# Attention and two squared-ReLU/mish MLPs on one core: tau and the first queries through ScalarE's queue, and a new written-out order

## The chip, the cores and the metric

The program runs on one core of a Trainium2 chip. The metric is device time in microseconds (us) of one execution; lower is better. The profile's engines are PE (TensorE), PEld (its weight loads), DVE (VectorE), ACT (ScalarE), POOL (GpSimd) and SP (SyncE, which here only issues DMAs). SPq and ACTq are the DMA issues in those engines' instruction streams.

## The reference

```python
# attention: 4 batches, 8 heads, 576 positions, head size 64
scores = scale * q @ k.T
scores = where(scores >= max(scores) - tau, scores, -1e9)     # tau = 0.02
attn = softmax(scores) @ v                                    # eps 1e-9 in the sum
x = attn as 2304 rows of 512
# first MLP, 512 -> 2048 -> 512
r = maximum(x @ w_in, 0);  x = (r * r) @ w_out
# second MLP, 512 -> 2048 -> 512
h = x @ w_in2;  out = (h * tanh(softplus(h))) @ w_out2
```

The inputs of the MLPs' weights are 64-bit floats, which the kernel reads as pairs of 32-bit words and takes apart into a high and a low 32-bit part.

## The kernel before, in words

Attention works on pairs of heads, four pairs in a batch, sixteen in all. A pair is of kind "d" (direct, fp32 throughout: all four of batch 0 and the first of batch 1), "h" (direct scores, values in two fp16 parts) or "s" (everything in two fp16 parts; ten pairs). `job_direct` loads a direct pair's k and q with two or three DMAs each, turns them on PE (the line L860 transposes into a PSUM tile `s`), and copies them to SBUF (L871 on ACT, L873 on DVE). `job` does the same for an "s" pair: its loads of k and q are of the kind "n4", four DMAs each (L768, L770), into the buffers `f0` to `f2`, and its turns are DMA transposes (L488). `unit` takes two head tiles of scores: matmuls L491 into `s0` and `s1`, then on DVE `top` (L936), which scales by `cd` and finds the maximum, then `most` (n<-m, L946 on ACT, L951 on DVE), then exp on ACT, with the mask either on ACT (L973 and L977) or on DVE (L984 and L989). `cd` comes from tau through `consts` (L509 to L515 on DVE). In the fp16 pairs the weights of the attention go to `pt` by a DMA transpose (`pt<-hl`, L488) and the values' matmul is `small<-V,pt`.

The attention's rows go to DRAM (xs: `xdr<-xx`, L1160) and come back as the MLP's blocks (xl: `xx<-xdr`, L1249). There are nine blocks of 256 rows. The first MLP of seven blocks runs between the attention's units; from about 500 us on PE does MLP work alone. The weights of the first MLP are loaded by `weights` (L548, L556) and converted by five to seven operations for each half: `size` L581, `rest` L593, `clamp` L588, `shift` L605, `sign` L611 (or, where `sp` says so, `factor` and `times`), `to_hi` and `to_lo` (L650).

Nothing of the order is left to the framework. Every operation and every DMA is put into a `Plan` with its possible engines, their costs, its dependencies and a due time. `Plan.order` runs a list scheduling forwards and backwards `fbi` times over a model of the engines, and the kernel issues everything in the order of the starts so found; each engine then runs its own instructions in that order and waits at each for what it needs. The parameters in `PAR` and `BIAS` set due times (`cd`, `blk`, `off`, `ahead`), which spare places are used (`ex`, `exo`), how a choice of engine is biased (`BIAS`), how late a load is taken to land after its issue (`land`), when PE prefers to stay with fp16 or fp32 (`stayt`, `stay`), and which queues a kind of DMA may use (`on`: S for SP, A for ACT). `LOADS` holds each kind's issue cost in each queue. `warm` puts up to eight matmuls of `ones` into PE's gaps at the start. `pm` says how many of nine score tiles have their mask on ACT, for each batch.

Of the kernel before, what the change touches and what calls it, by code (L numbers as in the profile page):

```python
# [24 lines left out]


PAR = dict(
    on=dict(n3="S", n4="S", x2="A", xl="SA", xs="A"),
    merge=8,
    warm=(1, 0, 7),  # L30
    won=("S", "S"),
    land=1.963,
    lag=0.625,
    turns=("h", "s0"),
    kv=(("nat0", "V1"), ("f1", "nat1"), ("KT1", "f0"), ("V0", "KT0")),
    cd=(-308.461, 3.819, -131.904),
    urg=-14.633,
    rawt=-5.99,
    kinds="dddd",
    cgen=4.726,  # L40
    split=(),
    ex=dict(cw=3, cr=2, raw=37, pd=6, sc=1),
    exo=("sc", "cr", "cw", "pd", "raw"),
    blk=list((8.563, 55.919, 139.126, 253.351, 384.4, 475.303, 619.227, 867.985, 1044.55)),
    tb2=83.369,
    down2=308.21,
    sp=(0, 4),
    off=(175.279, 19.269, 48.635, -244.561, 181.854, 84.18, -264.447, -32.298),
    ahead=(25.339, 120.493, 7.244, -166.185, 20.703, 130.933, 10.735, 565.487, 305.271, -75.571),
    start=-133.597,  # L50
    area=dict(sc=("x0", "x1"), hl=("x2",)),
    jobahead=21.48,
    fbi=7,
    stay=1.5,
    stayt=150.0,
    kinds2="ssss",
    kb=("dhss", "ssss", "ssss"),
    pm=(9, 9, 3, 0),
    tmax=0.75,
    pstay=4.0,  # L60
    proom=0.7,
)


# [20 lines left out]
class Plan:  # L85
# [3 lines left out]


    TABLE = 1.3
    BIAS = {"V": 2.013, "A": 1.855, "P": 2.0, "S": 0.46}
    SHARE = 0.8
    FIRST = 0.4
    TICK, ENTRY = 3.4133, 1.275
# [21 lines left out]
    def op(self, opts, fn, r=(), w=(), x=(), due=0.0, load=None, tab=None, two=False, half=0):  # L117

        o = Op()
        o.two, o.half, o.bank = two, half, 0  # L120
        for b in (*r, *w, *x):
            o.bank |= b.bank
        o.opts, o.fn, o.due, o.load, o.tab, o.n = opts, fn, due, load, tab, len(self.ops)
        deps = set()
        for b in r:
            assert b.wr and not b.gone, "read before written or after its place's next use"
            deps.update(b.wr)
            b.rd.append(o.n)
        for b in w:
            for z in b.prevs:  # L130
                deps.update(z.users())
            b.wr.append(o.n)
        for b in x:
            deps.update(b.users())
            b.wr.append(o.n)
        deps.discard(o.n)
        o.deps = deps
        self.ops.append(o)
        return o
# [77 lines left out]
    def forwards(self, succ):  # L217
# [29 lines left out]
        while count < len(ops):  # L247
            best = None
            for e in engs:
# [8 lines left out]
                for _, n in now:  # L258
                    o = ops[n]
                    if len(o.opts) > 1:  # L260
                        bias = self.BIAS
                        mine = t + o.opts[e] + bias[e]
# [110 lines left out]
def attention_moe_moe_kernel(ctx: ExitStack, tc: tile.TileContext, q, k, v, tau, w1i, w1o, w2i, w2o, out):  # L373
    nc = tc.nc
    B, H, S, D = q.shape
# [15 lines left out]
    tt = sb.tile([128, 6], F32, name="tt", tag="tt")  # L391
    cd = sb.tile([128, 8], F32, name="cd", tag="cd")
# [28 lines left out]
    def sbuf(place, shape, dt):  # L421
        if place in AREA or place in HALF:
            base, z, whole, over = HALF[place] if place in HALF else ("area", *AREA[place])
            n = min(whole, math.prod(shape[1:]) * (2 if dt == F16 else 4) // 4)

            def make():
                t = within(base, SIZE[base])[:, z:z + n]
                t = t if dt == I32 else t.bitcast(dt)
                if len(shape) == 4:
                    return t.rearrange("p (a b c) -> p a b c", b=shape[2], c=shape[3])  # L430
                return t.rearrange("p (a b) -> p a b", b=shape[2]) if len(shape) == 3 else t

            return plan.buf(place, make, over=over)
        return plan.buf(place, lambda: sb.tile(shape, dt, name=place, tag=place))
# [24 lines left out]
    def rot(*places):  # L459
# [5 lines left out]

    LOADS = {
        "n4": (dict(S=2.95, P=2.75, A=1.9), 1.86, 0.8, 1.9),
        "d3": (dict(S=2.05, P=2.1), 1.3, 0.5, 1.2), "d2": (dict(S=1.4, P=1.5), 0.65, 0.5, 0.8),
        "q1": (dict(S=0.75, P=0.8), 0.0, 0.4, 0.4), "q2": (dict(S=1.45, P=1.4), 0.62, 0.19, 0.65),
        "w8": (dict(S=0.6, P=0.9, A=0.5), 0.0, 3.4, 3.2),  # L470
        "w": (dict(S=0.6, P=0.75, A=0.45), 0.0, 1.8, 1.42), "n3": (dict(S=2.3, P=2.0, A=1.4), 1.24, 0.9, 1.6),
        "n2": (dict(S=1.45, P=1.35), 0.62, 0.5, 1.4),
        "tau": (dict(S=0.5, P=0.6), 0.0, 0.2, 0.2),
        "xs": (dict(S=0.72, P=0.65, A=0.5), 0.0, 0.36, 0.36), "tail": (dict(S=1.6, P=1.3), 0.6, 0.19, 0.38),
        "xl": (dict(S=0.63, P=0.56, A=0.45), 0.0, 0.55, 0.5), "x2": (dict(S=0.6, P=0.56, A=0.45), 0.0, 0.75, 0.7),
        "xr": (dict(S=0.45, P=0.56), 0.0, 0.64, 0.64), "out": (dict(S=0.45, A=0.45), 0.0, 0.65, 0.65),
# [3 lines left out]
    def dma(fn, kind, r=(), w=(), x=(), due=0.0, on=None):  # L480

        cost, *load = LOADS[kind]
        on = on or PAR["on"].get(kind, "S")
        op({e: cost[e] for e in on}, lambda e: fn({"S": nc.sync, "A": nc.scalar, "P": nc.gpsimd}[e]), r, w, x, due,
           load=load)
# [10 lines left out]
    blk = PAR["blk"]  # L496
    blk = blk + [blk[-1] + PAR["tb2"] * (n + 1) for n in range(NB + 1)]
# [6 lines left out]
    K, K0, KI, KT_ = (plan.buf(z, lambda: None) for z in ("const", "ones", "ident", "tau"))  # L504
# [10 lines left out]
        nc.vector.tensor_copy(out=cd[:, 3:4], in_=tt[:, 0:1])  # L515


    dma(lambda e: e.dma_start(out=tt[:, 3:4], in_=tau.to_broadcast([128, 1])), "tau", w=[KT_], due=-40.0)
    op({"V": 0.45}, consts, r=[KT_], w=[K], due=-39.0)

    W = {}
# [306 lines left out]
    def job_direct(p, due):  # L828

        keep = p.keep  # L830
        p.c, p.cv = K, None
        p.QT = sbuf(rot("Q0", "Q1"), [128, 576], F32)
        todo = [(q, p.QT, 6, p.tiles)]
        if keep is not None and "KT" in keep:
            p.KT = keep["KT"]
        else:
            p.KT = sbuf(rot("KT0", "KT1") if keep is None else PAR["kv"][p.h0 // 2][0], [128, 576], F32)
            todo.insert(0, (k, p.KT, 6.5, (0, 5)))
        for x, dst, z, (j0, j1) in todo:
            src = x[p.b, p.h0:p.h0 + 2]  # L840
            raw = sbuf(rot(*(spare["raw"] if not p.late else ("f0", "f1", "f2"))), [128, 5, 2, 64], F32)
            main = min(j1, 4)

            def load(e, raw=raw, x=src, j0=j0, j1=j1, main=main):
                for h in range(2):
                    e.dma_start(
                        out=raw()[:, j0:main, h, :],
                        in_=x[h, 0:512, :].rearrange("(p j) d -> p j d", j=4)[:, j0:main, :],
                    )
                if j1 == 5:  # L850
                    e.dma_start(out=raw()[0:64, 4, :, :], in_=x[:, 512:576, :].rearrange("h p d -> p h d"))

            dma(load, "d3" if main - j0 == 4 else "d2", w=[raw], due=due - 9 - z)
            o = pbuf(place("s", "s0", "s1"), [128, 1024])
            cols = slice(128 * j0, min(576, 128 * j1))

            def turn(e, raw=raw, o=o, j0=j0, j1=j1):
                for j in range(j0, j1):
                    n = 128 if j < 4 else 64
                    nc.tensor.transpose(  # L860
                        o()[:, 128 * j:128 * j + n], raw()[0:n, j].rearrange("p h d -> p (h d)"), ident[0:n, 0:n]
                    )

            t = op({"T": 0.15 * (j1 - j0)}, turn, r=[raw, KI], w=[o], due=due - z)
            if len(turns) < 2:
                turns.append(t)
                warm(len(turns), t)

            def evac(e, dst=dst, o=o, cols=cols):
                if e == "A":  # L870
                    nc.scalar.activation(out=dst()[:, cols], in_=o()[:, cols], func=AF.Copy)  # L871
                else:
                    nc.vector.tensor_copy(out=dst()[:, cols], in_=o()[:, cols])  # L873

            n = cols.stop - cols.start
            op({"A": 0.11 + 0.42 * n / 576, "V": 0.1 + 0.6 * n / 576}, evac, r=[o], w=[dst], due=due - z + 1 - URG)

        if keep is not None and "V" in keep:
            p.V = keep["V"]
            return  # L880
        if p.kind == "h":
            return job_v(p, due)
        p.V = V = sbuf(rot("V0", "V1") if keep is None else PAR["kv"][p.h0 // 2][1], [128, 10, 64], F32)
        if keep is not None:
            keep.update(KT=p.KT, V=p.V)


        def load_v(e):
            r = V().rearrange("p (h j) d -> p h j d", h=2)
            vv = v[p.b, p.h0:p.h0 + 2]  # L890
            e.dma_start(
                out=r[:, :, 0:4, :].rearrange("p h j d -> p h (j d)"),
                in_=vv[:, 0:512, :].rearrange("h (p j) d -> p h (j d)", j=4),
            )
            e.dma_start(out=r[64:128, :, 4, :], in_=vv[:, 512:576, :].rearrange("h p d -> p h d"))

        dma(load_v, "n2", w=[V], due=due - 8)
# [727 lines left out]
    with tc.manual_schedule():  # L1625
        made, code = {}, nc.cur_bb.bb.instructions
        followed = {o.after for o in plan.ops if o.after is not None}
        for n in seq:
            o = plan.ops[n]
            z = len(code)  # L1630
# [39 lines left out]
```

## Time and profile before

| | |
|---|---|
| time, median of 3 runs | 1012.12 us (1010.97 to 1012.97) |
| profiled execution | 1012.55 us, of which the span of its instructions is 1010.8 us |
| PE busy | 987.2 us, 98% of the span |
| DVE, ACT, POOL busy | 649.6, 523.8 and 86.4 us |
| mean granted clock of PE | 0.997 |

The span runs from the first to the last instruction; 1.75 us lie around it. Busy time of PE counts matmuls whose ends are modelled, and issuing a DMA does not count as busy time of the engine that issues it.

### The profile page before, as it was taken

Reading aid. Unit: us, or ns where it says so; the run is one execution under the profiler, and the core shown is the slowest. Engines: PE = TensorE matmul, PEld = TensorE weight load, DVE = VectorE, ACT = ScalarE, POOL = GpSimd, SP = SyncE. Lnnn points to the kernel's source line nnn. Section 1 sums busy time; section 2 is a strip of 40 time slices with the busy share of each in tenths; the row PEclk is TensorE's granted clock in tenths of the full one; section 3 lists DMA queues with packets and bytes.
Section 4 is the critical chain, followed back from the end, with each engine's and each line's share of the span. In section 5 each row is a group of like instructions: output and inputs, shape, how many; then the busy total and the mean of one; then the engine's idle time right before and its main releaser. Section 6 shows DMA issues by size and latency. Waiting matters only on the chain.

```text
span 1010.8 us, 20772 instructions
## 1 busy us (share of the span) xinstructions
PE 987.2 (98%) x8191; PEld 863.4 (85%) x8191; DVE 649.6 (64%) x1486; ACT 523.8 (52%) x978; POOL 86.4 (9%) x120
## 2 busy tenths in 40 slices
PE   6899999999999999999999999999999999999998
PEld 4577799889888898998999888888888888888997
DVE  4999999888898897889855799943223122222222
ACT  5899988867777665766544578611111120111111
POOL 1344312100000100110001000000000000000000
PEclk8999999999999999999999999999999999999999
DMA  7635667897978797779852345401011010010001
GB/s 206 201 119 161 200 130 159 159 162 152 177 142 153 145 171 144 139 158 150 158 163 78 108 153 172 168 1 42 1 42 42 0 42 1 21 42 1 1 12 51
DMA packets 231185, 109.43 MB, mean 108 GB/s; under 512 B 194608, under 2 KB 212016, under 8 KB 231088
## 3 DMA queue, kind: packets, MB, share of 16 engines
q1 hardware_dynamic: 219504, 98.93, 43.7%
q10 hardware_dynamic: 11584, 9.18, 2.9%
q8 instruction: 64, 1.05, 0.4%
q14 instruction: 33, 0.27, 0.1%
HBM read 58.16 MB, written 14.16 MB: 72 GB/s over the span
## 4 chain that ended last, share of the span: by engine, by line
PE 80%; DMA 4%; SPq 2%; DVE 1%; ACT 1%; issue 0%; ACTq 0%
PE s L491 27%; PE acc L491 24%; PE h L491 19%; PE small L491 9%; DMA pt<-hl 2%; SPq L488 1%; DMA f<-in_q_dram 1%; SPq L770 1%; SPq L768 0%; DMA pt<-area 0%; PE s L1254 0%; DMA xx<-xdr 0%; DVE gl L650 0%; PE s L1372 0%; DVE e L989 0%
## 5 line engine op out<-in xcount | busy, mean ns | idle before, releaser
L491 PE MATMUL acc<-gh,wo 128*128 128x256 f32 (+1 forms) x960 | 190.0, 287 | 0.0
L491 PE MATMUL h<-xh,wi 128*128 128x256 f32 x896 | 167.6, 279 | 0.0
L491 PEld LDWEIGHTS acc<-gh,wo 128*128 128x128 f32 x960 | 154.7, 192 | 4.1 <-issue 2.1
L491 PEld LDWEIGHTS h<-xh,wi 128*128 128x128 f32 x896 | 142.6, 192 | 2.5 <-issue 1.8
L491 PE MATMUL acc<-gl,wo 128*128 128x256 f32 (+1 forms) x480 | 135.3, 282 | 0.0
L491 PE MATMUL h<-xo,wi 128*128 128x256 f32 x448 | 123.3, 275 | 0.8 <-DVE xo L1271 0.8
L491 PEld LDWEIGHTS acc<-gl,wo 128*128 128x128 f32 x480 | 92.0, 192 | 0.9
L491 PE MATMUL s<-KT,area 64*128 64x512 f16 (+7 forms) x840 | 86.2, 331 | 3.0 <-DVE hl L936 2.5
L491 PEld LDWEIGHTS h<-xo,wi 128*128 128x128 f32 x448 | 86.0, 192 | 1.0 <-DVE xo L1271 1.0
L936 DVE TENSOR_SCALAR_CACHE_REDUCE area<-s,c 128x576 f32<-128x576 f32 x90 | 70.8, 811 | 7.7 <-PE s L491 7.6
L491 PE MATMUL acc<-wo,gh 128*128 128x512 f32 x216 | 73.9, 379 | 0.0
L643 DVE CAST gh<-pt 128x512 fp32r<-128x512 f32 x17 | 7.3, 427 | 97.5 <-PE small L491 92.0
L977 ACT ACTIVATE e<-e,tt 128x576 f32<-128x576 f32 x84 | 64.6, 770 | 0.9 <-DVE xx L1137 0.4
L491 PE MATMUL s<-KT,wi 128*128 128x512 f32 x192 | 64.9, 379 | 0.0
L491 PE MATMUL s<-f,wi 128*128 128x512 f32 x192 | 64.9, 379 | 0.0
L643 DVE CAST gh<-area 128x512 fp32r<-128x512 f32 x18 | 7.7, 426 | 88.1 <-PE small L491 82.4
L650 DVE TENSOR_TENSOR gl<-r,gh 128x512 fp32r<-128x512 f32 x83 | 57.5, 693 | 3.6 <-ACT gh L639 2.8
L491 PE MATMUL small<-V,pt 128*128 128x64 f16 (+1 forms) x1540 | 54.8, 194 | 4.2 <-DMA pt<-hl 3.9
L1462 ACT ACTIVATE r<-s 128x512 f32<-128x512 f32 x18 | 10.8, 598 | 91.5 <-PE s L491 90.1
L491 PEld LDWEIGHTS <-pt 128*128 128x128 f16 (+1 forms) x1540 | 45.9, 101 | 14.1 <-issue 6.8
L989 DVE SCALAR_TENSOR_TENSOR e<-area,n,e 128x576 f32<-128x576 f32 x60 | 48.1, 810 | 14.9 <-ACT e L984 14.5
L491 PE MATMUL s<-hl,wi 128*128 128x512 f32 (+1 forms) x192 | 56.6, 344 | 0.0
(321 smaller groups left out, 2233.6 us busy)
## 6 DMA issues: line engine op xcount, KB each, us to landing
area<-in_moe_w_out_dram SPq DMA_DIRECT2D x30, 512.0 KB, 4.1
area<-in_moe_w_in_dram SPq DMA_DIRECT2D x20, 512.0 KB, 4.3
x2dr<-stg ACTq DMA_DIRECT2D x18, 256.0 KB, 4.1
xx<-xdr SPq DMA_DIRECT2D x34, 128.0 KB, 2.5
xdr<-xx ACTq DMA_DIRECT2D x32, 128.0 KB, 3.2
wi<-in_moe_w_in_dram SPq DMA_DIRECT2D x6, 512.0 KB, 4.1
wo<-in_moe_w_in_dram SPq DMA_DIRECT2D x6, 512.0 KB, 3.8
f<-in_q_dram SPq DMA_DIRECT2D x24, 128.0 KB, 3.6
```

Source lines behind the costliest of these rows:

```text
L488: dma(lambda e: e.dma_start_transpose(out=dst(), in_=src()), "turn", r, w, due=due)
L491: nc.tensor.matmul(o, l, r, start=start, stop=stop, skip_group_check=True)
L643: nc.vector.tensor_copy(out=o, in_=i)
L650: VEC[e].tensor_tensor(out=part(lo), in0=src(), in1=f32(part(hi)), op=ALU.subtract)
L770: e.dma_start(out=raw[64 * a:64 * a + 64, :, 4, :], in_=x[:, 512:576, :].rearrange("h p d -> p h d"))
L936: nc.vector.tensor_scalar(out=sc(), in0=s()[:, 0:576], scalar1=c()[:, 3:4], scalar2=None, op0=ALU.mult, op1=ALU.min, accum_out=m()[:, i:i ...
L977: nc.scalar.activation(out=ex(), in_=ex(), func=AF.Exp, bias=tt[:, 5:6], accum_out=l()[:, 0, u:u + 1])
L989: nc.vector.scalar_tensor_tensor(out=ex(), in0=sc(), scalar=nt()[:, i:i + 1], in1=ex(), op0=ALU.is_le, op1=ALU.mult, accum_out=l()[:, 0, u ...
L1462: nc.scalar.activation(out=out, in_=in_, func=AF.Mish)
```

## The change

tau and the q of the first pair get the queue "A" and a due time ahead of all others. The loads of kind "n4" go from SP's queue to ACT's; x2 and xs may now use either queue, xl only SP's. The planner takes loads to land 1 us later (`land`), and all searched parameters are new ones, so every engine's instructions may stand in another order. The first of the two halves of each of the first MLP's eight input chunks takes `factor` (ACT) and `times` (DVE or POOL) for `sign` (`sp`), one score tile of nine in batch 1 moves its mask from ACT to DVE and one in batch 2 the other way (`pm`), and POOL's bias goes from 2.0 to -10.755 while the room that POOL asks for beside DVE (`proom`) goes from 0.7 to 1.0.

```diff
-    on=dict(n3="S", n4="S", x2="A", xl="SA", xs="A"),
+    on=dict(n3="S", n4="A", x2="SA", xl="S", xs="SA"),
-    land=1.963,
-    lag=0.625,
+    land=2.967,
+    lag=0.175,
-    cd=(-308.461, 3.819, -131.904),
-    urg=-14.633,
-    rawt=-5.99,
+    cd=(-310.29, 15.769, -136.476),
+    urg=-21.291,
+    rawt=-11.32,
-    cgen=4.726,
+    cgen=2.071,
-    ex=dict(cw=3, cr=2, raw=37, pd=6, sc=1),
-    exo=("sc", "cr", "cw", "pd", "raw"),
+    ex=dict(cw=6, cr=1, raw=41, pd=3, sc=1),
+    exo=("cw", "sc", "cr", "pd", "raw"),
...
-    sp=(0, 4),
+    sp=(1, 0),
...
-    stayt=150.0,
+    stayt=300.0,
-    pm=(9, 9, 3, 0),
+    pm=(9, 8, 4, 0),
-    pstay=4.0,
-    proom=0.7,
+    pstay=1.0,
+    proom=1.0,
...
-    BIAS = {"V": 2.013, "A": 1.855, "P": 2.0, "S": 0.46}
+    BIAS = {"V": 2.249, "A": 1.959, "P": -10.755, "S": 0.46}
...
-        "d3": (dict(S=2.05, P=2.1), 1.3, 0.5, 1.2), "d2": (dict(S=1.4, P=1.5), 0.65, 0.5, 0.8),
+        "d3": (dict(S=2.05, P=2.1, A=1.5), 1.3, 0.5, 1.2), "d2": (dict(S=1.4, P=1.5, A=1.0), 0.65, 0.5, 0.8),
-        "tau": (dict(S=0.5, P=0.6), 0.0, 0.2, 0.2),
+        "tau": (dict(S=0.5, P=0.6, A=0.5), 0.0, 0.2, 0.2),
...
-    dma(lambda e: e.dma_start(out=tt[:, 3:4], in_=tau.to_broadcast([128, 1])), "tau", w=[KT_], due=-40.0)
+    dma(lambda e: e.dma_start(out=tt[:, 3:4], in_=tau.to_broadcast([128, 1])), "tau", w=[KT_], due=-1e3,
+        on="A")
...
-            dma(load, "d3" if main - j0 == 4 else "d2", w=[raw], due=due - 9 - z)
+            first_q = x is q and p.b == 0 and p.h0 == 0 and j0 == 0
+            dma(load, "d3" if main - j0 == 4 else "d2", w=[raw], due=-2e3 if first_q else due - 9 - z,
+                on="A" if first_q else None)
```

The due times `blk`, `tb2`, `down2`, `off`, `ahead`, `start` and `jobahead` are new numbers too.

## Rows read from the trace of the kernel before

**Rows 1.** Busy time by stage: stretch, length, each engine's busy us (instructions), clock, DMA share, GB/s.

```profile
0.00:50.00 50.00, 38.93 (x276) 26.72 (x278) 34.65 (x85) 35.38 (x74) 12.17 (x21) 0.93 0.73 204
50.00:100.00 50.00, 49.88 (x483) 34.99 (x480) 49.98 (x133) 48.62 (x104) 20.37 (x27) 1.00 0.45 137
100.00:300.00 200.00, 197.09 (x2305) 173.29 (x2304) 182.35 (x457) 159.09 (x317) 28.34 (x41) 1.00 0.79 160
300.00:500.00 200.00, 194.73 (x2439) 176.47 (x2438) 170.13 (x444) 132.17 (x243) 18.71 (x26) 1.00 0.83 151
500.00:1004.00 504.00, 504.00 (x2686) 450.02 (x2685) 212.45 (x371) 147.34 (x239) 6.83 (x6) 1.00 0.18 59
```

**Rows 2.** Timeline, all engines, first 15 us: start, length, instruction, [idle before <-releaser].

```profile
0.72 1.38 SPq L846 DMA_DIRECT2D wo<-in_k_dram  x2
...
2.81 1.28 SPq L846 DMA_DIRECT2D wo<-in_q_dram  x2
...
4.28 1.38 PE L860 MATMUL s<-ident,wo 128*128 128x128 f32 x5 [2.00 <-DMA wo<-in_k_dram]
...
5.45 0.43 SPq L518 DMA_DIRECT2D tt<-in_tau_dram  x1
5.70 0.65 ACT L871 ACTIVATE KT<-s 128x576 f32<-128x576 f32 x1 [3.69 <-PE s L860]
...
6.39 1.38 PE L860 MATMUL s<-ident,wo 128*128 128x128 f32 x5 [0.73 <-DMA wo<-in_q_dram]
...
9.28 1.84 PE L491 MATMUL s<-KT,area 64*128 64x512 f32 x8
...
10.57 0.15 DVE L509 TENSOR_SCALAR tt<-tt 128x1 f32<-128x1 f32 x1 [10.57 <-DMA tt<-in_tau_dram]
...
13.40 0.81 DVE L936 TENSOR_SCALAR_CACHE_REDUCE hl<-s,cd 128x576 f32<-128x576 f32 x1
```

**Rows 3.** Busy time of three stretches of the start, columns as in rows 1.

```profile
10.00:12.00 2.00, 2.00 (x16) 1.40 (x12) 1.36 (x7) 0.00 (x0) 0.00 (x0) 1.00 0.95 372
12.00:14.00 2.00, 0.21 (x2) 0.02 (x1) 1.37 (x3) 1.40 (x3) 0.00 (x0) 1.00 1.21 297
...
17.90:24.30 6.40, 6.40 (x24) 4.55 (x26) 5.27 (x10) 4.52 (x10) 1.43 (x3) 0.52 0.84 239
```

**Rows 4.** Costliest groups of the page: xcount | busy us, mean ns of one | idle before, releaser.

```profile
L491 PE MATMUL small<-V,pt 128*128 128x64 f16 (+1 forms) x1540 | 54.8, 194 | 4.2 <-DMA pt<-hl 3.9
```

**Rows 5.** Timelines of SP, PE and ACT around 335 us.

```profile
334.88 1.29 SPq L770 DMA_DIRECT2D f<-in_k_dram  x2
336.34 1.29 SPq L488 DMA_TRANSPOSE pt<-hl  x1
...
341.42 0.58 PE L491 MATMUL small<-V,pt 128*128 128x64 f16 x14 [1.52 <-DMA pt<-hl]
...
332.04 0.55 ACTq L1160 DMA_DIRECT2D xdr<-xx  x1
332.63 0.78 ACT L984 ACTIVATE e<-area,m 128x576 f32<-128x576 f32 x1 [3.91 <-DMA f<-in_q_dram]
```

**Rows 6.** DMA issues by line: xcount, shortest/median/longest ns, first and last start.

```profile
L1160 ACTq DMA_DIRECT2D xdr<-xx x32: 520/528/572, 51.7 to 508.4; - x32
L768 SPq DMA_DIRECT2D f<-in_q_dram x20: 582/637/1832, 105.3 to 439.8; - x20
```

**Rows 7.** Groups by line: xcount | busy us, mean ns of one | idle before, releasers.

```profile
L650 POOL TENSOR_TENSOR gl<-r,gh 128x512 fp32r<-128x512 f32 x7 | 9.1, 1295 | 37.0 <-ACT nat L694 13.1 <-DVE e L989 9.2 <-DVE l L1006 6.2
L650 DVE TENSOR_TENSOR gl<-r,gh 128x512 fp32r<-128x512 f32 x83 | 57.5, 693 | 3.6 <-ACT gh L639 2.8
L984 ACT ACTIVATE e<-area,m 128x576 f32<-128x576 f32 x60 | 45.3, 765 | 11.5 <-DMA f<-in_q_dram 3.9 <-DMA pt<-area 3.0 <-DVE area L936 1.6
```

**Rows 8.** Chain that ended last, in order of time: start, us, what.

```profile
150.97 1.34 PE acc L491 x12
152.74 1.42 PE acc L491 x12
```

More of the change, by code (lines that the diff above doesn't have):

```diff
@@ L31 @@
     won=("S", "S"),
-    land=1.963,
-    lag=0.625,
+    land=2.967,
+    lag=0.175,
     turns=("h", "s0"),
     kv=(("nat0", "V1"), ("f1", "nat1"), ("KT1", "f0"), ("V0", "KT0")),
-    cd=(-308.461, 3.819, -131.904),
-    urg=-14.633,
-    rawt=-5.99,
+    cd=(-310.29, 15.769, -136.476),
+    urg=-21.291,
+    rawt=-11.32,
     kinds="dddd",
-    cgen=4.726,
+    cgen=2.071,
     split=(),
-    ex=dict(cw=3, cr=2, raw=37, pd=6, sc=1),
-    exo=("sc", "cr", "cw", "pd", "raw"),
-    blk=list((8.563, 55.919, 139.126, 253.351, 384.4, 475.303, 619.227, 867.985, 1044.55)),
-    tb2=83.369,
-    down2=308.21,
-    sp=(0, 4),
-    off=(175.279, 19.269, 48.635, -244.561, 181.854, 84.18, -264.447, -32.298),
-    ahead=(25.339, 120.493, 7.244, -166.185, 20.703, 130.933, 10.735, 565.487, 305.271, -75.571),
-    start=-133.597,
+    ex=dict(cw=6, cr=1, raw=41, pd=3, sc=1),
+    exo=("cw", "sc", "cr", "pd", "raw"),
+    blk=list((39.965, 87.471, 170.279, 256.506, 409.416, 507.736, 643.738, 889.802, 1050.198)),
+    tb2=82.608,
+    down2=396.1,
+    sp=(1, 0),
+    off=(179.923, 17.316, -30.023, -283.334, 149.329, 58.913, -272.69, -48.24),
+    ahead=(25.294, 166.197, 8.206, -165.347, 20.705, 184.366, 18.289, 478.782, 355.62, -160.604),
+    start=-110.41,
     area=dict(sc=("x0", "x1"), hl=("x2",)),
-    jobahead=21.48,
+    jobahead=19.785,
     fbi=7,
     stay=1.5,
-    stayt=150.0,
+    stayt=300.0,
     kinds2="ssss",
     kb=("dhss", "ssss", "ssss"),
-    pm=(9, 9, 3, 0),
+    pm=(9, 8, 4, 0),
     tmax=0.75,
-    pstay=4.0,
-    proom=0.7,
+    pstay=1.0,
+    proom=1.0,
 )
```

## The prediction

> **What bounds the kernel now.** I read busy time by stage first. From 500 to 1004 us PE is busy for all of 504.0 us, so nothing that the change does to DVE, ACT or the queues can show there unless it makes PE wait; I take that half as fixed. From 50 to 100 us three engines are full at once, PE 49.88, DVE 49.98 and ACT 48.62 of 50. From 100 to 500 us PE is idle for 2.91 + 5.27 = 8.18 us in all [rows 1]. The one part with a visible hole is the first 50 us: 38.93 of 50 busy, 11.07 us idle, at a mean clock of 0.93. The time is therefore PE's work plus PE's gaps: 11 us at the start, 8 us in the middle, and what the clock costs. The change adds no matmul and takes none away, apart from the few on ones, so it can only move gaps, the clock and PE's changes between fp16 and fp32.
>
> Next I read the start's timeline. SP issues k first (0.72 us), then q (2.81), then, behind a weight, tau (5.45). k is turned at 4.28, q at 6.39 after 0.73 us of waiting; the first scores stand at 9.28 and end at 11.12. DVE has nothing until tau lands at 10.57, and, after `consts`, does not start its first `top` before 13.40; what it does in between is weight conversions [rows 2]. PE is busy for 0.21 of the 2 us from 12 to 14 while the scores wait for that `top`, and afterwards, from 17.9 to 24.3 us, it runs at a granted clock of 0.52, the lower of its two levels, 1.2 GHz [rows 3].
>
> Last the middle's waits. The largest item is `small` waiting for the transposes `pt<-hl`, 3.9 us [rows 4]. One of these waits shows how it comes about: a transpose starts at 336.34, right after the issues of a k load of kind "n4" in SP's queue, and PE waits 1.52 us for it at 341.42 [rows 5].
>
> **The change part by part.** *tau and the first q on ACT.* SP's first issues become k and then weights. On ACT three issues for q and one for tau cost about 4 x 0.53 = 2.1 us by ACT's own issues [rows 6]. ACT has nothing else to do before it copies k out at 5.70 [rows 2], so I cost them at nothing; without that idle time they would push the copy by those 2.1 us. From its first issue to its turns q took 6.39 - 2.81 = 3.58 us, and k 4.28 - 0.72 = 3.56; issued at 0.72, q is there at about 4.3. Then PE turns k from 4.28 to 5.66 and q to 7.04; with 0.65 for the copy [rows 2] and some 0.3 for the handovers the scores start at 8.0 and not at 9.28: 1.3 us. They take 1.84, so `top` can start at 9.9, against 13.40: 3.5 us. tau took 5.12 us from issue to use; issued by 2.8 it is there by 8, before the scores end, so it is no longer what comes last. Late next is either the scores or the weights, whose conversions stood ahead of `top`. They have to be done at some time, and DVE is full from 50 us on; below 3.5 us the gain is limited by how many of them the new order leaves ahead. Bounds 0 (another load or DVE's backlog holds the second unit) and 3.5; I take the middle of 1.3 and 3.5, **-2.4 us**. PE, DVE and ACT are all full right behind this stretch, so a start that is earlier on all three is passed on to PE.
>
> One rule speaks against this part. k and q now move at the same time; together the DMA engines show at most 372 GB/s at the start [rows 3]. The Trainium skill (DMA: Bandwidth & Descriptors, section "Issuing engines are not separate DMA queues") says that DMAs of all issuing engines run on the same 16 DMA engines and interleave. By that rule only the issue time of q is saved, and k may land later; the trace of before, in which all early loads are on one queue, can't show it. What the kernel would then do is worked out under the rivals.
>
> *The clock.* PE's stretch at half speed, 6.4 us, follows the hole from 12 to 14 us [rows 3]. If the hole closes and the clock stays up, at most 6.4 / 2 = 3.2 us come back; if another hole opens, nothing. How much of the stretch is PE's own work can't be seen, so I take a fifth, **-0.6**, with both ends, 0 and 3.2, for the range.
>
> *n4 from SP to ACT.* Twenty loads of four issues leave SP: 80 x 0.637 = 51 us of its time between 105 and 440 us; they cost ACT 80 x 0.528 = 42 us [rows 6]. ACT has 200 - 159.1 + 200 - 132.2 = 109 us not busy in that stretch [rows 1], so the issue time itself fits; were that cover gone, the 42 us would go straight onto the exps. What SP loses is the kind of issue that stands ahead of the transposes: I take away two such waits, 2 x 1.52 = -3.0 of the 3.9. What ACT gains is a new risk: an issue that has to wait stops the exps behind it. The trace has such a case: ACT stands still for 3.91 us, its x store goes out at 332.04, and the exp behind it starts at 332.63 [rows 5]. Another wait of 3.0 us before the same kind of exp was put down to a transpose [rows 7]. A wait on ACT holds exp, then the high and low parts, the transpose and `small`. I give back 1.9 of the 3.0: **-1.1**, with bounds from -6 (three quarters of the 8.18 us go) to +8 (as much again).
>
> *land, lag, due times, places.* These move everything and price nothing by themselves. They are inside the bounds just given. Loads taken to land 1 us later should stand earlier in their queues; the tau row, 5.12 us from issue to use [rows 2], says that an early issue is what the start wants.
>
> *stayt 150 to 300.* From 150 to 300 us PE no longer prefers to stay with one type. Twelve fp32 matmuls take 1.42 us after a run of another type and 1.34 otherwise [rows 8]; with as much at the way in, a change and back costs about 0.16 to 0.2 us. The 1540 value matmuls [rows 4] are 110 runs of 14, as the one at 341.42 [rows 5], nearly all between 130 and 500 us, some 45 in those 150 us; if a third of them stands apart anew, that is 15 x 0.2 = 3.0. No change in their number gives 0; the planner prices changes itself, so I stay near the lower end: **+0.6**.
>
> *sp, pm, POOL's bias.* Eight `sign` operations leave DVE, and ACT and POOL or DVE get two operations for each; four score masks go to DVE and four to ACT. A piece of work that goes to POOL takes 1.295 us for DVE's 0.693 [rows 7]. DVE's time in the middle, 47.5 us not busy from 100 to 500 [rows 1], and the weights' due times, long before their matmuls, hide these: 0, and where the cover is gone about 0.6 us for each piece that PE waits for, which the range's ends take in.
>
> The sum is -2.4 - 0.6 - 1.1 + 0.6 = -3.5. From the profiled execution's 1012.55 that is 1009.05; the median of the runs is 0.43 lower, so **1008.6 us**.
>
> **The rivals.** *The start is not passed on.* Weights and the second pair's loads set the pace from 10 to 24 us, where the DMA share is 0.84 to 1.21 in the stretches shown [rows 3], and the early `top` only waits longer later. Against it: DVE's 10.57 us without work are followed by full engines. Then 1012.1 - 1.1 + 0.6 = 1011.6, no difference.
>
> *ACT's queue stalls the exps (slower).* Issues on ACT rise by up to 80 from 52 (32 x stores [rows 6], the rest x2 stores and two reads). With 52 there were 3.9 + 3.0 = 6.9 us of ACT standing still for DMAs [rows 7]; 80 more at that rate are 10.6 us. In the case at 332 us PE lost 1.52 of ACT's 3.91 [rows 5], 39%; at 60%, in a denser queue, PE loses 6.4, and nothing is won at the transposes: 1012.1 - 2.4 - 0.6 + 0.6 + 6.4 = 1016.1. It decides from the point where PE's new waits pass 2.4 us (start, clock and types together), and shows as slower past 4.4. For it: loads wait for free `f` buffers, and on SP such waits cost nothing. Against it: ACT's 109 us of room.
>
> *The shared DMA engines take back part of the start.* k's transfer and q's share what the engines move: q's 2 x 576 x 64 x 4 B = 295 KB at 372 GB/s [rows 3] add 0.8 us to k. Turns from 5.1, scores at 8.8, `top` at 10.7: between 0.5 and 2.7, the middle 1.6 us instead of 2.4, and 1009.4 in all. This is the case of the Trainium skill's rule above (DMA: Bandwidth & Descriptors).
>
> *The new order closes most gaps.* The middle gives 6 us, the rest as forecast: 1012.1 - 2.4 - 0.6 - 6 + 0.6 = 1003.7.
>
> **How the numbers follow.** Chances: forecast 0.43, start not passed on 0.18, ACT's queue 0.18, shared DMA engines 0.10, most gaps closed 0.11. About 0.2%, 2 us, is what a measurement of this kernel can tell from no change: faster is below 1010.1, slower above 1014.1. Faster: 0.39 of the forecast, 0.11, and 0.08 of the shared engines, 0.58. Slower: 0.16 of ACT's queue and 0.05 out of the tails of the forecast and of the start, 0.21. The rest is 0.21. The range goes to the case of closed gaps with the clock's full 3.2 at its low end (1003.7 - 2.6 = 1001.1, rounded up to 1001.5) and to ACT's queue at its high end, 1016.
>
> **What would show it.** In the changed kernel's profile: q's and tau's issues on ACT from 0.72 us; q's turns right behind k's, without a wait; the first scores near 8.0 and `top` near 9.9, not 13.4; PE's idle time in the first 50 us at 8 to 9 us instead of 11; fewer or shorter stretches at the lower clock; PE's waits for `pt<-hl` at 1 to 2 us; 80 issues at L768 and L770 on ACT, with the exps' waits for DMAs not above some 10 us in all. I would be wrong if k is turned clearly after 4.3 us, if DVE still does weights while scores stand ready, if waits on ACT appear ahead of the transposes between 130 and 500 us, or if PE's busy time past 500 us gains any gap.

## The result, and the profile after

The changed kernel takes 1022.28 us in the median of four runs, the kernel before 1012.08. One of the four, 1127.5 us at a mean clock of 0.851, is left out of the ratio, which is 1.0093, 95% interval 1.0066 to 1.012; the median of the other three is 1020.98. It is slower, where 1008.6 was forecast. The profiled execution took 1020.98 us with a span of 1019.2, 8.4 more than before.

Busy time by stage of the changed kernel, columns as in [rows 1]:

```profile
0.00:50.00 50.00, 42.25 (x332) 29.20 (x334) 38.93 (x107) 39.78 (x83) 8.84 (x16) 1.00 0.79 213
50.00:100.00 50.00, 47.89 (x459) 33.72 (x456) 49.70 (x131) 49.71 (x110) 12.88 (x16) 1.00 0.46 139
100.00:300.00 200.00, 193.57 (x2221) 170.08 (x2219) 178.07 (x446) 153.85 (x306) 23.28 (x29) 1.00 0.78 155
300.00:500.00 200.00, 192.09 (x2404) 173.26 (x2403) 174.04 (x453) 126.67 (x231) 24.14 (x37) 0.99 0.81 149
500.00:1004.00 504.00, 503.68 (x2740) 449.68 (x2739) 170.26 (x275) 202.91 (x332) 20.38 (x19) 1.00 0.20 61
```

Against [rows 1], PE's gaps in the first 50 us fall from 11.07 to 7.75 us and the clock there is 1.00 and not 0.93. From 50 to 100 us they rise from 0.12 to 2.11, from 100 to 500 from 8.18 to 14.34, and after 500 to 0.32. In sum 24.52 against 19.37, 5.15 us more. The other 3.3 us are PE's own busy time, 990.5 against 987.2, for the same 8191 matmuls. The slower clock doesn't explain them: the changed kernel loses less to it, as the stretches below show. 2.4 us of them are there in the run `a_plan_sp` too (989.6), so most of it belongs to the new order; what in it stays open.

PE's waits in the changed kernel: line, releaser, us in all, times, longest:

```profile
PE s L491 <- DVE xo L1274: 4.5, 1, 4.5
PE s L863 <- DMA wo<-in_q_dram: 2.8, 1, 2.8
PE h L491 <- ACT r L1302: 2.6, 2, 1.3
...
PE small L491 <- DMA pt<-hl: 0.3, 1, 0.3
```

The waits for the transposes, 3.9 us in [rows 4], are nearly gone. In their place stand others. The longest, 4.5 us, is put down to DVE; the chain that ended last shows what DVE waited for (start, us, what):

```profile
298.29 7.30 DMA pt<-hl
305.59 0.02 issue
305.61 0.57 ACTq L769
306.18 0.04 issue
306.22 0.65 ACTq L771
306.86 0.04 issue
306.90 0.64 ACTq L771
307.54 0.05 issue
307.59 0.60 ACT xh L1269
```

and ACT's timeline the same stretch (start, length, instruction, idle before):

```profile
299.41 6.77 ACTq L769 DMA_DIRECT2D f<-in_k_dram  x2
306.22 1.32 ACTq L771 DMA_DIRECT2D f<-in_k_dram  x2
307.59 0.60 ACT L1269 ACTIVATE xh<-s 128x512 fp32r<-128x512 f32 x1 [7.97 <-issue]
```

A k load of kind "n4" has four issues on ACT. After the first, the second waits until 305.61 for a transpose of SP's queue that landed at 305.59. The trace's records of the issues show why the two are tied: all DMAs of SP and ACT carry eight semaphores by turns, 62 or 63 DMAs each. None of the 431 issues whose forerunner on the same semaphore has a recorded landing starts before that landing, whichever engine issued the forerunner. ACT's computing stands still for 7.97 us; `xh`, which comes from ACT, is late, and so is DVE's `xo`, which makes PE wait. The hole has an echo in PE's clock (columns as above):

```profile
300.00:310.00 10.00, 5.52 (x59) 4.86 (x59) 4.09 (x9) 2.41 (x5) 1.23 (x3) 0.98 1.15 175
310.00:320.00 10.00, 10.00 (x125) 8.70 (x122) 8.76 (x24) 8.22 (x17) 1.25 (x3) 0.85 0.36 74
```

PE is busy for 5.52 of 10 us, and in the next 10 the granted clock is 0.85 on average, some 3 us at the lower of its two levels, 1.2 GHz. With the 0.98 of the stretch before that is 1.7 us lost to the clock. The kernel before lost more, 3.5 us, in its first 50 us (0.93 on average, [rows 1]).

The start went otherwise than forecast (timeline):

```profile
0.72 1.36 ACTq L847 DMA_DIRECT2D wo<-in_q_dram  x2
0.72 1.63 SPq L847 DMA_DIRECT2D wi<-in_k_dram  x2
...
5.08 1.38 PE L863 MATMUL s<-ident,wo 128*128 128x128 f32 x5 [2.79 <-DMA wo<-in_q_dram]
...
6.08 0.15 DVE L509 TENSOR_SCALAR tt<-tt 128x1 f32<-128x1 f32 x1 [6.08 <-DMA tt<-in_tau_dram]
...
6.39 1.41 PE L863 MATMUL s<-ident,wi 128*128 128x128 f32 x5
...
7.73 1.65 PE L491 MATMUL acc<-ones 128*128 128x128 f32 x6
...
7.84 0.65 ACT L874 ACTIVATE KT<-s 128x576 f32<-128x576 f32 x1 [0.69 <-PE s L863]
...
9.31 2.40 PE L491 MATMUL s<-KT,area 64*128 64x512 f32 x8
...
11.48 0.69 DVE L606 SCALAR_TENSOR_TENSOR stg<-stg,area 128x512 int32<-128x512 int32 x1
...
12.09 0.81 DVE L939 TENSOR_SCALAR_CACHE_REDUCE hl<-s,cd 128x576 f32<-128x576 f32 x1
```

q and k are issued together, and the first turns, now q's, start at 5.08 and not at 4.28. The first scores stand at 9.31, where [rows 2] have 9.28. In both kernels six matmuls of `ones` (`warm`) stand on PE right in front of them; before:

```profile
7.70 1.65 PE L491 MATMUL acc<-ones 128*128 128x128 f32 x6
```

In the changed kernel the last copy, `KT`, is done at 8.49, and the scores start 0.8 us later, when the `ones` end. Only `top` comes earlier, 12.09 against 13.40: tau is there at 6.08, and what DVE does right before `top` is a weight's conversion (L606).

### The profile page after: what moved, and what is told of

Its sections match the earlier page's. It is cut to its first block, busy times and chain, and to the rows that moved or that the text cites. A ratio compares the mean times of both kernels' runs of the same rounds, so it can differ in the third digit from the quotient of the medians.

```text
span 1019.2 us, 20769 instructions
## 1 busy us (share of the span) xinstructions
PE 990.5 (97%) x8191; PEld 865.3 (85%) x8191; DVE 612.4 (60%) x1411; ACT 575.4 (56%) x1065; POOL 89.5 (9%) x116
## 4 chain that ended last, share of the span: by engine, by line
PE 67%; ACT 10%; DVE 9%; DMA 7%; issue 3%; ACTq 2%; SPq 1%; DVEq 0%
PE s L491 24%; PE acc L491 20%; PE h L491 15%; PE small L491 8%; ACT e L976 3%; DMA pt<-hl 3%; ACT e L980 2%; DMA f<-in_q_dram 1%; ACTq L771 1%; DVE area L939 1%; DVE e L992 1%; DMA area<-in_moe_w_in_dram 1%; DMA xx<-xdr 1%; DMA area<-in_moe_w_out_dram 1%; DVE hl L939 1%
## 5 line engine op out<-in xcount | busy, mean ns | idle before, releaser
L651 DVE TENSOR_TENSOR gl<-pt,gh 128x512 fp32r<-128x512 f32 x17 | 11.8, 692 | 138.2 <-ACT gh L640 138.2
L640 ACT ACTIVATE gh<-r 128x512 fp32r<-128x512 f32 x68 | 42.7, 628 | 33.2 <-PE small L491 20.9
L491 PE MATMUL s<-xh,wi 128*128 128x512 f32 (+1 forms) x192 | 56.7, 345 | 0.2 <-ACT pt L1465 0.2
L1021 DVE TENSOR_TENSOR hl<-e,hl 128x512 f16<-128x512 f32 (+1 forms) x111 | 53.9, 495 | 2.3 <-ACT hl L1016 2.1
```

The costliest lines, as they stand in the source:

```text
L491: nc.tensor.matmul(o, l, r, start=start, stop=stop, skip_group_check=True)
L640: nc.scalar.activation(out=o, in_=i, func=AF.Copy)
L651: VEC[e].tensor_tensor(out=part(lo), in0=src(), in1=f32(part(hi)), op=ALU.subtract)
L1021: VEC[e].tensor_tensor(out=hl()[:, a:a + n], in0=ex()[:, z:z + n], in1=hl()[:, z:z + n], op=ALU.subtract)
```

## The experiments

Two theories at first. Theory 1: the n4 loads on ACT stop the exps behind them. Theory 2: the new order is worse whoever issues the loads, as any order might be that wasn't settled on with its own parameters. Theory 3, later: the loss is in the other new parameters. Each ratio is to the kernel before on the same chip, with its 95% interval.

**Moving the issues and keeping both orders.** `a_n4_sp` and `b_n4_act` change only who issues:

```diff
-        op({e: cost[e] for e in on}, lambda e: fn({"S": nc.sync, "A": nc.scalar, "P": nc.gpsimd}[e]), r, w, x, due,
+        queue = {"S": nc.sync, "A": nc.scalar, "P": nc.gpsimd}
+        op({e: cost[e] for e in on}, lambda e: fn(nc.sync if kind == "n4" else queue[e]), r, w, x, due,
```

(`a_n4_sp` in the changed kernel; `b_n4_act` in the kernel before, with `nc.scalar`.)

> The changed kernel's order, every instruction in its place, but the n4 loads of k and q issued by SP. Theory 1 (ACT's queue): the 80 issues on ACT wait for earlier DMAs and stop the exps behind them; without them ACT's standing still in front of those issues goes, the 4.5 us wait at 305 us goes, and the time falls by 5 to 9 us to 1013 to 1017. Theory 2 (the order itself): the new order is worse wherever the loads are issued; the time stays at 1019 to 1024, or rises because SP was not planned to have the loads.

> The kernel before, every instruction in its place, but the n4 loads issued by ACT where SP issued them. Theory 1: ACT stands still for the waits of 80 issues and the time rises by 5 to 15 us. Theory 2: ACT has over 100 us of room between 100 and 500 us and the order is the good one; within 3 us of 1012.

Measured: `a_n4_sp` 1.0205 (1.018 to 1.0229), slower still; `b_n4_act` 1.0201 (1.017 to 1.0232), about 20 us slower. The second bears theory 1 out, and by more than its 5 to 15 us. The first misses by theory 1; a rise is what theory 2 allowed for. PE's waits in `a_n4_sp` are

```profile
PE small L492 <- DMA pt<-hl: 7.8, 6, 1.8
PE s L1258 <- DMA xx<-xdr: 5.9, 4, 2.8
PE small L492 <- DMA pt<-area: 4.5, 2, 2.4
```

All three are waits for DMAs that SP issues: the transposes and the x blocks. I take it that SP, for which the new order leaves no time for 80 more issues (it has most x stores too), is late with them. Putting the loads back without planning for them is no test of the move; either queue charges for them.

In `b_n4_act` ACT hardly waits in front of the issues. Two groups of them (times, shortest/median/longest ns, first and last start):

```profile
L769 ACTq DMA_DIRECT2D f<-in_q_dram x20: 568/635/1202, 104.4 to 459.8; - x20
...
L771 ACTq DMA_DIRECT2D f<-in_k_dram x18: 625/699/1102, 165.4 to 453.6; - x18
```

By my sum over ACT's timeline the 80 issues take 55.1 us there, and ACT stands still in front of them for 1.0 us. In the changed kernel they take 55.4 us, and ACT stands still in front of them for 21.1.

**Planning them anew.** `b_plan_act` is the kernel before with n4="A", `a_plan_sp` the changed kernel with n4="S", both with the order planned for it (the edit of `b_plan_act`; `a_plan_sp` has n4="S" for n4="A"):

```diff
-    on=dict(n3="S", n4="S", x2="A", xl="SA", xs="A"),
+    on=dict(n3="S", n4="A", x2="A", xl="SA", xs="A"),
```

> The kernel before with one parameter changed, n4 on ACT, and planned anew, so that the planner knows of the issues on ACT. If the move itself costs (theory 1, narrowed: what counts is ACT standing still, not that the order was made for another queue): 1017 to 1025, like the changed kernel. If the move is harmless when planned (theory 3: the loss is in the other new parameters): 1009 to 1015.

> The changed kernel with n4 back on SP and planned anew. Theory 1: 1008 to 1015, no exps stopped behind loads. Theory 3: 1018 to 1026, since the due times and places stay the new ones.

Measured: `b_plan_act` 1.0251 (1.0229 to 1.0273), 1038.27 us and so beyond theory 1's range; `a_plan_sp` 1.0006 (0.9992 to 1.002), 1014.06 us and within it. One word decides: with it on SP, all the rest of the change together is worth nothing that can be told from zero, and with it on ACT the old parameters lose 25 us. Theory 3 falls. PE's gaps from 100 to 500 us in `a_plan_sp` are 7.87 us, against the changed kernel's 14.34:

```profile
100.00:300.00 200.00, 196.23 (x2259) 171.75 (x2260) 180.91 (x449) 162.84 (x325) 23.02 (x32) 1.00 0.80 157
300.00:500.00 200.00, 195.90 (x2459) 177.06 (x2458) 174.19 (x451) 134.32 (x244) 19.36 (x27) 1.00 0.88 152
```

With the changed kernel's other parameters the move costs about 9 us and not 25. One difference is at hand: there x2 and x stores may go to SP, and ACT issues 92 DMAs in all, against 130 in `b_plan_act`. No run tests that by itself.

**A new plan by itself.** `b_land` takes only `land` and `lag` into the kernel before:

```diff
-    land=1.963,
-    lag=0.625,
+    land=2.967,
+    lag=0.175,
```

> The kernel before planned anew with land 2.967 and lag 0.175 and nothing else; n4 stays on SP. Theory 2 (any order that wasn't settled on with its own parameters loses): 1017 to 1026. Theory 1 alone (only ACT's queue costs): within 3 us of 1012.

Measured: 0.9977 (0.9962 to 0.9993), 1010.71 us. Theory 2 falls: a new plan with n4 on SP loses nothing; by this interval it gains some 2 us.

> The same kernel as b_land, one more look for its trace on this chip: within 0.3% of its 1010.7.

Measured: 1013.04 us in one run, 0.23% above 1010.7, on a chip where the kernel before takes 1012.81. It shows no gain.

**The start by itself.** `b_start` keeps the order before, but issues q and tau first, on ACT:

```diff
+        if act:
+            early.insert(0, o.n)
...
+    seq = early + [n for n in seq if n not in early]
```

> The kernel before, its order kept, but tau and the first q issued first of all, on ACT. The forecast's first step by itself: 1.5 to 3.5 us faster (1009 to 1010.5). Rival: k and q land later together, as in the changed kernel, where the first scores still stood at 9.31 us; then only the earlier tau helps, and the gain is 0 to 1.3 us.

Measured: 0.9991 (0.9976 to 1.0007), no difference that can be told. Its timeline:

```profile
5.82 2.73 PE L866 MATMUL s<-ident,wo 128*128 128x128 f32 x10 [3.54 <-DMA wo<-in_k_dram]
7.84 0.15 DVE L514 TENSOR_SCALAR tt<-tt 128x1 f32<-128x1 f32 x1 [7.84 <-DMA tt<-in_tau_dram]
10.05 1.80 PE L496 MATMUL s<-KT,area 64*128 64x512 f32 x8
11.89 0.82 DVE L942 TENSOR_SCALAR_CACHE_REDUCE hl<-s,cd 128x576 f32<-128x576 f32 x1 [0.58 <-PE s L496]
```

k is turned 1.5 us later than alone, the scores start 0.8 us later than before, and only `top` gains 1.5 us: the rival of this expectation.

**The issues on a third engine.** `a_n4_pool` keeps the changed kernel's order and lets POOL issue n4 (`nc.gpsimd if kind == "n4"`).

> The changed kernel's order, every instruction in its place, but the n4 loads issued by POOL, which has little to do from 130 to 500 us, so that neither the exps nor the transposes stand behind them. Theory 1: the waits in front of the exps go, 1011 to 1017, unless issuing from POOL is itself dear. Theory 3: no gain, 1019 to 1026.

Measured: 1.0068 (1.0046 to 1.009). The median, 1019.24 us, misses theory 1's 1011 to 1017; the interval overlaps the changed kernel's own 1.0066 to 1.012, so whether anything was gained can't be told. PE's 4.5 us wait at 305 us is gone; busy time there (columns as in [rows 1]):

```profile
300.00:310.00 10.00, 9.44 (x116) 8.53 (x116) 7.53 (x17) 5.55 (x12) 3.48 (x7) 1.00 1.14 202
```

PE's gaps from 100 to 500 us are 10.0 us and not 14.3, but the mean clock of this profiled execution is 0.993, the changed kernel's 0.998. And ACT waits 12.0 us for the loads to land:

```profile
ACT nat L696 <- DMA f<-in_k_dram: 8.2, 3, 4.2
...
ACT nat L696 <- DMA f<-in_q_dram: 3.8, 4, 1.3
```

**Issue time or waits.** What is dear on ACT, the time that four issues take (theory 1a), or the waits in front of them (theory 1b)? `b_dummy` puts ACT's time where the loads stand, without a DMA; `b_n4_one` and `b_n4_two` move one and two of four issues (the diff of `b_n4_one` is shown; `b_n4_two` has `nc.scalar` for both values of `h`); the order is that of before in all three.

```diff
+            def load(e, raw=raw, x=x):
+                natural(e, raw().rearrange("p j (h d) -> p h j d", h=2), x)
+                for _ in range(10):
+                    nc.scalar.activation(out=junk, in_=ones[:, 0:64], func=AF.Copy)
```

```diff
-            e.dma_start(out=raw[:, h, 0:4, :], ...
+            (nc.scalar if h == 0 else e).dma_start(out=raw[:, h, 0:4, :], ...
```

> The kernel before, order kept, loads on SP as before, but ACT does ten small copies (128 x 64, about 0.2 to 0.25 us each) at each of the 20 places where an n4 load stands: ACT's time for four issues without a DMA and without its waits. It adds to the reference's work and changes no result. Theory 1a (ACT's time is what is dear, it has no room where the loads stand): 8 to 20 us slower, like b_n4_act. Theory 1b (the waits in front of the issues are what is dear): within 3 us of before.

> The kernel before, order kept, with only the first of the four issues of each n4 load on ACT and three on SP: a quarter of the issue time on ACT, but the wait for the buffer and for earlier DMAs is still in front of it. Theory 1a: 3 to 6 us slower. Theory 1b: 10 to 20 us slower, nearly all of b_n4_act's 19.

> The kernel before, order kept, with the two 128 KB issues of each n4 load on ACT and the two 32 KB ones on SP: half of ACT's issue time. One issue of four cost nothing (0.998), four cost 19 us. Theory 1a (ACT's time, in proportion): 6 to 12 us slower. Rival (ACT has some room, and only the second pair of issues goes beyond it): within 3 us of before.

Measured: `b_dummy` 1.0254 (1.0225 to 1.0283); `b_n4_one` 0.9979 (0.9963 to 0.9994); `b_n4_two` 1.006 (1.004 to 1.008). The copies, by tile (times, shortest/median/longest ns), and the stages of `b_dummy`:

```profile
L784 ACT ACTIVATE junk<-ones x200: 239/256/261, 106.3 to 468.7; 128x64 f32<-128x64 f32 x100
```

```profile
100.00:300.00 200.00, 181.86 (x2057) 158.67 (x2055) 164.03 (x404) 168.22 (x390) 27.22 (x39) 0.98 0.74 148
300.00:500.00 200.00, 189.91 (x2352) 171.32 (x2352) 168.68 (x441) 154.71 (x347) 17.17 (x23) 1.00 0.79 148
```

The copies are 51.1 us of work. ACT's busy time from 100 to 500 us rises by 31.7 us over [rows 1], 322.9 against 291.3 (some of its other work now comes after 500), still 77 us short of full, and PE's gaps there rise from 8.2 to 28.2 us. No DMA was moved. So ACT's time alone, at these places, is enough for all of the loss in the order before: theory 1a. The 1.0 us of waits in `b_n4_act` says the same. The steps are not in proportion: with none, one, two and four of the four issues on ACT the ratios are 1, 0.998, 1.006 and 1.020. One issue is even a small gain, perhaps because SP loses a quarter of its own, which no run tests; the forecast of 3 to 6 us for it missed, and 1b's 10 to 20 us by more. For two, the 6 us lie at the edge of the proportional 6 to 12, and the rival's 3 us are too few.

**What loses nothing, together.** `b_land_tau` is `b_land` with tau alone first on ACT; `b_land_tau_one` adds the one issue of four.

> b_land (before planned anew with land 2.967 and lag 0.175, n4 on SP) with tau alone issued first on ACT and q left behind k on SP, so that k and q don't share the engines. If the shared landing is what kept b_start from its gain: 0 to 2 us below b_land, 1009 to 1011. If the start is not on the path: 1010.5 to 1012.

> The three edits that lost nothing together: planned anew with land 2.967 and lag 0.175, tau first on ACT, and the first of each n4 load's four issues on ACT. If their gains add: 1006 to 1009. If PE's work is the floor and they share one gain: 1010 to 1012, as b_land_tau.

Measured: 0.9979 (0.9964 to 0.9995), 1010.82 us, no gain over `b_land` that can be told; and 0.9955 (0.9941 to 0.9968), 1008.34 us, which beats both kernels. Its stages from 100 to 500 us:

```profile
100.00:300.00 200.00, 197.69 (x2308) 175.02 (x2307) 184.84 (x466) 156.26 (x305) 24.66 (x35) 1.00 0.79 158
300.00:500.00 200.00, 198.08 (x2510) 179.91 (x2508) 176.35 (x456) 127.32 (x229) 22.26 (x28) 1.00 0.87 156
```

PE's gaps there are 4.2 us, half of those in [rows 1]; `b_land` by itself has 5.7. Whether the one issue adds to `b_land_tau` stays open, as their intervals overlap.

## Why the prediction was wrong

**n4 from SP to ACT, forecast -1.1, is the step that failed.** Between `a_plan_sp` and the changed kernel it costs 1.0093 - 1.0006, some 9 us, about the end of its own bounds (+8), and with the old parameters 25. What the step took off for SP is borne out in part. In `b_n4_act`, where only the queue changes, PE's waits for `pt<-hl` fall from 3.9 to 1.6 us. In the changed kernel they are 0.3, but so they are in `a_plan_sp` with n4 on SP, which waits 3.8 us for `pt<-area` instead; and in `b_plan_act`, with n4 on ACT, they are 9.4.

What failed is the cover. The step held ACT's 109 us not busy against 42 us of issues and called them hidden. The size was low: it took an x store's 0.528 us for an issue, and the 80 took 55 us, with 21 us of standing still in front of them. But 76 us would still fit into 109. What was wrong is to count idle time as room. ACT's idle time from 100 to 500 us is mostly waiting for DVE (some 66 us) and for PE (some 20); the largest item of the kernel before is `most` waiting for `top` (line, releaser, us in all, times, longest):

```profile
ACT n L946 <- DVE area L936: 29.9, 22, 4.0
```

Behind each of these instructions stands the next link of scores, exp, transpose and values, and what is put in front of it delays it. `b_dummy` shows that 51 us of copies in that room cost PE 20 us of gaps from 100 to 500 us. Rows that were at hand hinted at it: DVE was at 182 of 200 us and PE at 197 [rows 1].

Three signs of being wrong that the prediction set came true: the first turn stands at 5.08 us and k's at 6.39, PE has 0.32 us of gaps past 500, and exps waited for the landing of n4 loads for 12.0 us and behind issues for 11.3, where some 10 in all were allowed.

**The rival that named ACT's queue** was right in the place, with a chance of 0.18 and 1016.1 us. Its mechanism was the waits, 10.6 us of them on ACT, of which PE would lose 6.4. The changed kernel has 21.1 us of them, and PE's gaps from 100 to 500 us lie 6.5 us above those of `a_plan_sp`. That the sizes are so near is partly luck: the share of 60% was a guess, and it also used the wait of 1.52 us at 341.42, which the step itself had put down to SP's queue. The one gap at 305 us is 4.5 us, and of ACT's 7.97 us there 5.6 are the wait and 2.3 the issues. In the order before, on the other hand, the issue time does it all. How the 9 us of the changed kernel divide into issue time and waits stays open: `a_n4_pool` takes away both and brings late loads in their place.

**The start, forecast -2.4.** The scores didn't gain 1.3 us; they stand at 9.31, and q and k landed together and later. The working also left out the six matmuls of `ones`, 1.65 us on PE between the turns and the scores: by its own 0.65 + 0.3 us the scores of the kernel before would stand at 8.7 and not at 9.28. (ACT also had a table load of 1.28 us at 0.72 us, taken for idle time; in the changed kernel it stands at 3.44 and holds nothing up.) The rule that was set against this step (the Trainium skill, DMA: Bandwidth & Descriptors, "Issuing engines are not separate DMA queues") agrees with both traces: k turned at 5.82 in `b_start` and q at 5.08 here, against k's 4.28 alone. I gave it 0.10; its 0.8 us for the shared transfer is what the changed kernel shows (5.1 forecast), and became 1.5 in `b_start`. By itself the step is worth nothing that can be told. The gaps of the first 50 us did fall by 3.3 us, in an order planned anew, and those from 50 to 100 us rose by 2.0.

**The clock, forecast -0.6.** The slow stretch from 17.9 to 24.3 us is gone, as hoped, and a new, shorter one came at 310 us behind the new hole: 3.5 us lost before, 1.7 after, so some 1.8 us came back, inside the bounds of 0 and 3.2.

**stayt, forecast +0.6.** By my count of the matmuls fp16 stands in 37 separate runs from 150 to 300 us against 33; at the 0.2 us taken for a run that is 0.8. `a_plan_sp` has 38 and is no slower than before. No run tested it by itself.

**sp, pm, POOL's bias, forecast 0.** `a_plan_sp` has them all and stands at 1.0006, which shows their sum with the rest and not each by itself. Past 500 us ACT has 203 us of work against 147 and DVE 170 against 212, with 0.32 us of gaps on PE: hidden, as taken.

## What to carry to other kernels

Time in which an engine is not busy is room only where nothing on the path stands behind what is put there; look at what the idle time waits for, and at who waits for the engine next, before calling added work hidden. A DMA's issue takes time of the engine that issues it, here some 0.64 us each on ACT, so a queue is chosen by what stands behind it: planned for, the 80 issues cost nothing that can be told on SP (1.0006), and on ACT 9 to 25 us. Moving part of a load's issues, one of four, lost nothing (0.998) where moving all lost 20 us.

## What was not expected of the hardware

One issue of a plain load took ACT 0.64 us in the median in `b_n4_act`, and 80 of them, 55 us spread over 358, cost 20 us. The Trainium skill (Perfetto Trace Analysis, "DMA Optimizations") says that balancing DMAs over the engines that can issue them may help if descriptor generation, which keeps the issuing engine busy, is the bottleneck. Whether that holds for SP here no run shows; in the kernel before it issued for 283 of the 400 us from 100 to 500. A quarter of the issues on ACT gave 0.998, and all of them 1.020. Two loads of 0.29 MB issued at the same instant on two queues delayed the first by 0.8 to 1.5 us at rates far from the 372 GB/s seen later: in the changed kernel 181, 212 and 205 GB/s in the third, fourth and fifth us, where the DMA share was 0.80, 0.94 and 0.98.
